# Windowed attention and a feed-forward block on one core: the score products of four heads issued as one group

## The chip, the core and the metric

The kernel runs on one core of one Trainium2 chip. The metric is the device time in microseconds (us) of one execution. The engines are TensorE (PE in the profile; its weight loads are PEld), VectorE (DVE), ScalarE (ACT), GpSimd (POOL) and SyncE (SP), which issues the DMAs. Each engine works through its own queue in the order in which the program issues to it.

## The reference

Attention in which a row sees 31 keys around it and, for each of the 24 blocks of 32 keys, one key (the maximum over the block) with the block's mean value; then layer norm and a two-layer feed-forward block on the result, in float32.

```python
def _attn_ref(q, k, v):                     # each (4, 8, 768, 64)
    B, H, S, D = q.shape
    block, window = (32, 16)
    nb = S // block
    scale = 1.0 / np.sqrt(D)
    k_sum = k.reshape(B, H, nb, block, D).max(axis=3)
    v_sum = v.reshape(B, H, nb, block, D).mean(axis=3)
    scores_l = scale * np.matmul(q, k.transpose(0, 1, 3, 2))
    mask_l = np.abs(pos[:, None] - pos[None, :]) < window
    scores_s = scale * np.einsum('bhsd,bhnd->bhsn', q, k_sum) + np.log(block)
    scores_l_m = np.where(mask_l, scores_l, -1000000000.0)
    a = softmax(np.concatenate([scores_l_m, scores_s], axis=-1))    # written out in full, with 1e-09 in the divisor
    return np.matmul(a, np.concatenate([v, v_sum], axis=2))

def _moe_ref(x, g_ln, w_ch1, w_ch2):        # x (4, 768, 512), w_ch1 (512, 2048), w_ch2 (2048, 512)
    xn = (x - mu) / np.sqrt(var + 1e-06) * g_ln
    return x + np.maximum(xn @ w_ch1, 0.0) @ w_ch2
```

Queries and keys are drawn eight times as large as the values. The result has the shape (4, 768, 512).

## The kernel before

The 4 x 768 rows are cut into 24 tiles of 128 rows, six for each batch. The eight heads of a tile are done in two half tiles of four heads, so there are 48 half tiles, numbered t; t = 0 to 11 are batch 0, t = 12 to 47 are batches 1 to 3. Two tiles (256 rows) make a group g of the feed-forward block, so there are 12 groups.

Batch 0 (`early_k`, `early_qk`, `early_transp`, `early_pv`) works in float32 while weights are loaded and converted. For t = 12 and up, `attend(t)` records these steps:

- `load_q(t)` brings the queries (buffer `qs`) and splits them into two float16 parts (`qhl`).
- `load_k(t, pr)`, once for each pair pr of heads, brings 184 key columns for each head into the single buffer `ksg`, has GpSimd put in the 24 block keys, has ScalarE make the high part `kh` and VectorE the low part `kl`. `kh` has one buffer for each pair, `kl` two in all.
- `qk(t, pr)` makes the scores of the two heads: two float16 products for each head, against `kh` and `kl`, into one PSUM tile `s` (two such tiles exist).
- `softmax(t, pr)`: VectorE adds the mask and finds the row minimum of the negated scores for each head, GpSimd scales the minimum (`mn`), ScalarE takes the exponential of each head.
- `load_v(t)`, `transp(t)` (the weights `p` in float16 parts, transposed by a DMA into `pT`) and `pv(t)` (twelve float16 products into PSUM `o`).

The feed-forward block is `g1(s)`, s = 8 g + j: 24 products of 256 columns into PSUM `h` (two runs of 12), then `g2(s)`: 12 products of 512 columns into the accumulators `a` of the group's two tiles (two runs of 6). Its operands are 32 bits wide (float32r).

The order in which all this is issued is not that of the code. `Plan.record` collects every instruction as an operation; instructions inside one `with pl.unit()` become one operation that is not broken up. `Plan.schedule` then lays the operations out on the engines with fixed costs, 24 times forwards and backwards, and `Plan.issue` keeps the layout whose modelled end is earliest and issues in that order. One draw of random numbers (`SEED`, `SPREAD = 2000.0`) shifts the first ranking by up to 2000 ns for each step. The model charges TensorE `SWITCH` = 93 ns where an operation differs from the one before it in `half`, which marks the score products of batch 0, whose contraction is 64 deep.

```python
if e == "tensor" and self.ops[i].half != half:
    half, t = self.ops[i].half, t + self.SWITCH
```

Every instruction is issued from one line of the helper, so the profile shows line 284 for all; the tile names tell them apart.

Of the kernel before, what the change touches and what calls it, by code (L numbers as in the profile page):

```python
# [16 lines left out]
F16 = mybir.dt.float16  # L17
# [7 lines left out]
P = 128  # L25
# [5 lines left out]
NC = 184  # L31
# [8 lines left out]
EH = 4  # L40
BS = 3
ROUNDS = 24
SEED, DRAWS = 2, 1
SPREAD = 2000.0
WARMQ = 4
WARMV = 4
# [17 lines left out]
class Plan:  # L64
# [58 lines left out]
    def record(self, engine, op, a, k):  # L123
        on_chip = lambda x: isinstance(x, bass.AP) and x.space != bass.MemoryType.DRAM
        outs = [x for x in (a[0], k.get("accum_out"), *a[7:8]) if on_chip(x)]
        ins = [x for x in (*a[1:7], *k.values()) if on_chip(x)]
        i, after = len(self.ops) - bool(self.joined), {}
        for aps, write in ((ins, False), (outs, True)):
            for x in aps:
                tile, *b = self.box(x)  # L130
                assert self.uses.get(tile, 1), tile
                if tile not in self.uses:
                    self.uses[tile] = []
                    if tile in self.prev:
                        for _, w, j in self.uses[self.prev[tile]]:
                            after[j] = after.get(j, False) or not w
                        self.uses[self.prev[tile]] = None
                elif tile in self.prev:
                    after.setdefault(self.uses[tile][0][-1], False)
                for c, w, j in self.uses[tile]:  # L140
                    if (write or w) and b[0] < c[1] and c[0] < b[1] and b[2] < c[3] and c[2] < b[3]:
                        after[j] = after.get(j, False) or not (write and w)
                self.uses[tile].append((b, write, i))
        busy, moving = self.cost(engine, op, a, k, ins, outs)
        columns = 0
        if engine == "tensor":
            columns = ({'matmul': 4, 'transpose': 2}[op] if ins[-1].dtype == F32 else 1) * math.prod(n for _, n in a[0].ap[1:]) * ins[0].ap[0][1] / P
        if self.joined:
            x = self.ops[i]
            x.calls.append((op, a, k))  # L150
            x.after.update(after)
            x.busy += busy
            x.columns += columns
        else:
            half = engine == "tensor" and ins[0].ap[0][1] == P // 2
            x = SimpleNamespace(engine=engine, calls=[(op, a, k)], after=after, busy=busy, moving=moving, columns=columns, stage=self.stage, port=self.port(engine, op, ins, outs), half=half)
            self.ops.append(x)
        x.after.pop(i, None)
        if self.joined is None:
            self.joined = True  # L160
# [44 lines left out]
    def schedule(self, rank, after, back):  # L205

        count = len(self.ops)
        before = [[] for _ in range(count)]
        left = [len(x) for x in after]
        for i, x in enumerate(after):  # L210
            for j, wait in x:
                before[j].append((i, wait))
        ready, start, end = [0.0] * count, [0.0] * count, [0.0] * count
        free = dict.fromkeys(self.ENGINES, 0.0)
        coming, waiting = ({e: [] for e in self.ENGINES} for _ in range(2))
        ring, warm, columns, tick = 0.0 if back else self.FIRST, False, 0.0, 0.0
        port, half = 0.0, False
        for i in range(count):
            if not left[i]:
                heapq.heappush(coming[self.ops[i].engine], (0.0 if back else 1000.0, i))  # L220
        for _ in range(count):
            t, e = min(
                (free[e] if waiting[e] else max(free[e], coming[e][0][0]), k)
                for k, e in enumerate(self.ENGINES)
                if waiting[e] or coming[e]
            )
            e = self.ENGINES[e]
            while coming[e] and coming[e][0][0] <= t:
                i = heapq.heappop(coming[e])[1]
                heapq.heappush(waiting[e], (rank[i], i))  # L230
            i = heapq.heappop(waiting[e])[1]
            busy, moving = self.ops[i].busy, self.ops[i].moving
            if self.ops[i].port:
                t = port = max(t, port)
                port += busy
            if e == "tensor" and self.ops[i].half != half:
                half, t = self.ops[i].half, t + self.SWITCH
            if e == "tensor" and not back:
                while t >= tick + self.TICK:
                    warm, columns, tick = columns >= 3200, 0.0, tick + self.TICK  # L240
                busy *= 1 if warm else 2
                at, per = t, self.ops[i].columns / busy
                while t + busy >= tick + self.TICK:
                    columns += (tick + self.TICK - at) * per
                    warm, columns, tick = columns >= 3200, 0.0, tick + self.TICK
                    at = tick
                columns += (t + busy - at) * per
            start[i], free[e], end[i] = t, t + busy, t + busy
            if e == "sync":
                ring = max(ring, t if back else t + busy + self.SETUP) + moving  # L250
                if back:
                    free[e] = max(free[e], ring)
                end[i] = ring + (self.SETUP + busy if back else 0)
            for j, wait in before[i]:
                ready[j] = max(ready[j], end[i] + wait)
                left[j] -= 1
                if not left[j]:
                    heapq.heappush(coming[self.ops[j].engine], (ready[j], j))
        return start, end
# [29 lines left out]
def body(ctx: ExitStack, tc, qt, qa, qe, kt, ks, va, vb, vs, g_ln, w1, w2, blocks, out):  # L289
# [8 lines left out]
    def psum(tag, name, shape):  # L298
        return pl.tile(pools[tag], shape, F32, tag, name, 2)
# [16 lines left out]
    nc = pl  # L316
# [187 lines left out]
    st = {}  # L504
# [43 lines left out]
            )  # L548

    @pl.step  # L550
    def qk(t, pr):
        qhl = st[t, "q"]
        kh, kl = st[t, "k", pr]
        ps = psum("s", f"s{t}_{pr}", [P, 2, NC])
        with pl.unit():
            for u in range(2):
                nc.tensor.matmul(ps[:, u, :], qhl[:, 2 * pr + u, :], kh[:, u, :], start=True, stop=False)
                nc.tensor.matmul(ps[:, u, :], qhl[:, 2 * pr + u, :], kl[:, u, :], start=False, stop=True)
        st[t, "s", pr] = ps

    @pl.step
    def softmax(t, pr):
# [54 lines left out]
    @pl.step  # L617
    def early_k(t):
        T, hh = divmod(t, 2)
        w = P * T  # L620
        for v in range(2):
            src, m, x = k0[2 * hh + v], bt["m", 0][:, 2 * hh + v], kx[t % 2][:, v]
            if v == 0:
                nc.scalar.copy(x[:, :NW], src[:, w : w + NW])
                nc.gpsimd.tensor_copy(x[:, P + BLK : P + BLK + NB], m)
            else:
                nc.scalar.copy(x[:, D:], src[:, w : w + P])
                nc.gpsimd.tensor_copy(x[:, : NW - P], src[:, w + P : w + NW])
                nc.gpsimd.tensor_copy(x[:, BLK : BLK + NB], m)
# [17 lines left out]
    @pl.step  # L647
    def early_transp(t, pr):
        p = st[t, "p"][:, 2 * pr : 2 * pr + 2].rearrange("p j c -> p (j c)")
        ps = psum("h" if t < EH else "s", f"pp{t}_{pr}", [P, 3, P])  # L650
        with pl.unit():
            for i in range(3):
                nc.tensor.transpose(ps[:, i, :], p[:, i * P : i * P + P], ident[:])
        e = work(f"v16_{pr}", f"pT{t}_{pr}", [P, 3, P])
        nc.scalar.copy(e[:], ps[:])
        st[t, "pt", pr] = e
# [205 lines left out]
    def attend(t):  # L862
        if t < NEARLY:
            early_k(t)
            early_qk(t)
            for pr in range(2):
                softmax(t, pr)
            for pr in range(2):
                early_transp(t, pr)
                early_pv(t, pr)  # L870
        else:
            load_q(t)
            for pr in range(2):
                load_k(t, pr)
                qk(t, pr)
                softmax(t, pr)
            load_v(t)
            transp(t)
            pv(t)
        if t % 2 and t < 8:  # L880
            norm(t // 2)

    def norm(T):
        ln(T)
        lnT(T)
# [26 lines left out]
    for t in range(NEARLY):  # L912
        if t % 2 == 0:
            fetch_tail(t // 2)
        attend(t)
# [13 lines left out]
    for t in range(8, 2 * TT + 1):  # L929
# [7 lines left out]
        b, i = divmod(t, 2 * NT)  # L937
# [66 lines left out]
```

## Time and profile before

| what | value |
|---|---|
| median of 3 runs | 683.55 us (682.82 to 685.04) |
| profiled execution | 682.88 us |
| its span, first to last instruction | 680.8 us |
| TensorE busy | 655.8 us (96%) |
| VectorE busy | 511.7 us (75%) |
| ScalarE busy | 369.8 us (54%) |
| GpSimd busy | 218.6 us (32%) |
| mean granted TensorE clock | 0.99 |

The profiled execution is 2.08 us longer than its span. A matmul's duration in the profile holds its way through the array, so neighbours overlap: what a product costs in a full queue is the distance from its start to the next one's start, and sums below are made of such distances. Times in a timeline are microseconds from the start of the span.

### The profile page before, as it was taken

The page shows a single profiled execution, that of the slowest core. Times are in us where ns is not written, and L with a number is a line of the kernel's source. Part 1 is how long each engine was busy: PE and PEld are TensorE (multiplying, and loading weights), DVE is VectorE, ACT ScalarE, POOL GpSimd, SP SyncE. Part 2 cuts the span into 40 slices and gives each one's busy share as a digit, 9 for nine tenths or more (in the row PEclk, how much of TensorE's full clock was granted, in tenths as well). Part 3 has the DMA queues.
Part 4 walks back from the last instruction along what each step waited for, and adds up shares of the span by engine and source line. Part 5 has one row for each costly group of instructions (what it writes and reads, how often), then busy time and mean ns, then how long its engine had stood idle before and what let it go on. Part 6 is the DMA issues. An engine that isn't in the chain of part 4 may idle for free.

```text
span 680.8 us, 13615 instructions
## 1 busy us (share of the span) xinstructions
PE 655.8 (96%) x4641; PEld 577.8 (85%) x4641; DVE 511.7 (75%) x1370; ACT 369.8 (54%) x970; POOL 218.6 (32%) x421
## 2 busy tenths in 40 slices
PE   9959999999999999989999999899999999999998
PEld 6748898888988987878988888798989888989997
DVE  3899989877566899879999888898998574742211
ACT  3936788475566766666666555666664434311110
POOL 4211200233333444634444354355343332310000
PEclk9959999999999999999999999999999999999999
DMA  9990564446564655655664544564543321210000
GB/s 304 362 350 28 147 214 121 146 138 183 141 164 121 176 139 128 170 151 150 172 141 126 141 102 101 126 146 103 144 108 81 84 79 35 55 24 1 32 1 31
DMA packets 109495, 87.89 MB, mean 129 GB/s; under 512 B 63218, under 2 KB 93938, under 8 KB 109427
## 3 DMA queue, kind: packets, MB, share of 16 engines
q1 hardware_dynamic: 109426, 87.04, 47.0%
q8 instruction: 36, 0.59, 0.4%
q14 instruction: 33, 0.26, 0.1%
HBM read 66.27 MB, written 6.29 MB: 107 GB/s over the span
## 4 chain that ended last, share of the span: by engine, by line
PE 43%; DVE 18%; DMA 13%; ACT 6%; issue 6%; POOL 2%; SPq 1%; ACTq 0%; POOLq 0%; DVEq 0%
PE h L284 20%; PE a L284 19%; DVE xn L284 4%; DMA ksg<-in_kt 4%; DMA bst<-in_vs 3%; DVE kl L284 2%; DMA bst<-in_qa 2%; ACT p L284 2%; DVE hl L284 2%; PE s L284 2%; PE o L284 1%; DVE p L284 1%; DVE v L284 1%; DVE vsum L284 1%; DVE x L284 1%
## 5 line engine op out<-in xcount | busy, mean ns | idle before, releaser
L284 PE MATMUL h<-xth,w 128*128 128x256 f32 x1536 | 301.3, 286 | 0.9 <-ACT xth L284 0.7
L284 PEld LDWEIGHTS h<-xth,w 128*128 128x128 f32 x1536 | 246.0, 190 | 4.1 <-ACT xth L284 1.1
L284 PE MATMUL a<-w,hh 128*128 128x512 f32 (+1 forms) x768 | 241.6, 396 | 0.0
L284 PE MATMUL h<-xtl,w 128*128 128x256 f32 x768 | 216.9, 282 | 0.8 <-POOL xtl L284 0.7
L284 PEld LDWEIGHTS a<-w,hh 128*128 128x128 f32 x768 | 135.4, 188 | 24.2 <-issue 0.9
L284 PE MATMUL a<-w,hl 128*128 128x512 f32 (+1 forms) x384 | 149.9, 390 | 0.2 <-DVE hl L284 0.2
L284 PEld LDWEIGHTS h<-xtl,w 128*128 128x128 f32 x768 | 145.8, 190 | 3.3 <-POOL xtl L284 1.0
L284 DVE SCALAR_TENSOR_TENSOR hl<-h,hh 128x512 fp32r<-128x512 f32 x96 | 65.7, 685 | 71.6 <-ACT hh L284 71.0
L284 ACT ACTIVATE hh<-h 128x512 fp32r<-128x512 f32 x96 | 56.5, 588 | 97.3 <-PE a L284 39.3
L284 ACT ACTIVATE p<-p,mn,sv 128x184 f32<-128x184 f32 x144 | 76.5, 532 | 57.7 <-POOL mn L284 57.5
L284 PEld LDWEIGHTS a<-w,hl 128*128 128x128 f32 x384 | 72.2, 188 | 16.9 <-DVE hl L284 0.6
L284 POOL TENSOR_TENSOR p<-p,p 128x512 f16<-128x512 f32 x72 | 71.6, 1002 | 39.6 <-ACT p L284 39.0
L284 DVE STREAM_TRANSPOSE xn<-xn 32x128 f32<-32x128 f32 x256 | 77.5, 303 | 4.5
L284 ACT ACTIVATE kh<-ksg,sv 128x368 f16<-128x368 f32 x72 | 43.2, 599 | 50.5 <-POOL ksg L284 39.3
L284 DVE SCALAR_TENSOR_TENSOR kl<-ksg,sv,kh 128x368 f16<-128x368 f32 x72 | 50.3, 699 | 20.8 <-ACT kh L284 20.0
L284 POOL TENSOR_SCALAR mn<-mn,sv 128x2 f32<-128x2 f32 x72 | 30.7, 427 | 78.5 <-DVE mn L284 69.1
L284 DVE CUSTOM_DVE_ANT_0 p<-s,mask 128x184 f32<-128x184 f32 x144 | 44.7, 340 | 9.9 <-PE s L284 9.2
L284 ACT ACTIVATE bst<-bst 128x384 f32<-128x384 f32 (+2 forms) x55 | 32.5, 590 | 26.8 <-DMA bst<-in_qa 11.6
L284 POOL COPY ksg<-ksum 128x48 f32<-128x48 f32 x72 | 18.8, 261 | 84.1 <-DMA ksg<-in_kt 66.1
L284 DVE SCALAR_TENSOR_TENSOR v<-vst,sv,v 128x256 f16<-128x256 f32 x72 | 42.5, 612 | 1.7 <-ACT v L284 1.2
L284 DVE SCALAR_TENSOR_TENSOR wf<-raw,wf 128x512 uint32<-128x512 uint32 x64 | 41.8, 680 | 0.0
L284 POOL TENSOR_TENSOR x<-x,rc 128x256 f32<-128x256 f32 x36 | 25.2, 699 | 47.6 <-DVE x L284 44.0
(106 smaller groups left out, 818.3 us busy)
## 6 DMA issues: line engine op xcount, KB each, us to landing
raw<-in_w SPq DMA_DIRECT2D x32, 512.0 KB
ksg<-in_kt SPq DMA_DIRECT2D x72, 184.0 KB
qs<-in_qt SPq DMA_DIRECT2D x72, 128.0 KB
out_x<-x SPq DMA_DIRECT2D x23, 256.0 KB
vst<-in_va SPq DMA_DIRECT2D x36, 128.0 KB
bst<-in_ks SPq DMA_DIRECT2D x20, 192.0 KB
bst<-in_qa SPq DMA_DIRECT2D x15, 256.0 KB
bst<-in_vs SPq DMA_DIRECT2D x20, 192.0 KB
```

The costliest lines, as they stand in the source:

```text
L284: getattr(getattr(nc, self.ops[i].engine), op)(*a, **k)
```

## The change

In `attend(t)`, for batches 1 to 3, the two `qk(t, pr)` become one `qk(t)` behind both `load_k`: its eight products are one unit, so nothing can stand between the first pair's and the second pair's, and both PSUM tiles `s` are taken together. The products themselves are the same. The planner's `half` gets three values: 1 for the score products of batch 0, 2 for other float16 products (`qk` and `pv`), 0 for the rest. 93 ns are now also charged where TensorE goes from float16 products to others, but not for the way in. The random seed goes from 2 to 8. Since the order of all engines comes out of the planner, all of them get a new order.

```diff
--- before.py
+++ after.py
@@ -40,7 +40,7 @@
 EH = 4
 BS = 3
 ROUNDS = 24
-SEED, DRAWS = 2, 1
+SEED, DRAWS = 8, 1
 SPREAD = 2000.0
 WARMQ = 4
 WARMV = 4
@@ -152,7 +152,7 @@
             x.busy += busy
             x.columns += columns
         else:
-            half = engine == "tensor" and ins[0].ap[0][1] == P // 2
+            half = engine == "tensor" and (1 if ins[0].ap[0][1] == P // 2 else 2 * (ins[-1].dtype == F16))
             x = SimpleNamespace(engine=engine, calls=[(op, a, k)], after=after, busy=busy, moving=moving, columns=columns, stage=self.stage, port=self.port(engine, op, ins, outs), half=half)
             self.ops.append(x)
         x.after.pop(i, None)
@@ -214,7 +214,7 @@
         free = dict.fromkeys(self.ENGINES, 0.0)
         coming, waiting = ({e: [] for e in self.ENGINES} for _ in range(2))
         ring, warm, columns, tick = 0.0 if back else self.FIRST, False, 0.0, 0.0
-        port, half = 0.0, False
+        port, half = 0.0, 0
         for i in range(count):
             if not left[i]:
                 heapq.heappush(coming[self.ops[i].engine], (0.0 if back else 1000.0, i))
@@ -234,7 +234,8 @@
                 t = port = max(t, port)
                 port += busy
             if e == "tensor" and self.ops[i].half != half:
-                half, t = self.ops[i].half, t + self.SWITCH
+                t += self.SWITCH if self.ops[i].half + half != 2 or not self.ops[i].half else 0
+                half = self.ops[i].half
             if e == "tensor" and not back:
                 while t >= tick + self.TICK:
                     warm, columns, tick = columns >= 3200, 0.0, tick + self.TICK
@@ -548,15 +549,16 @@
             )
 
     @pl.step
-    def qk(t, pr):
-        qhl = st[t, "q"]
-        kh, kl = st[t, "k", pr]
-        ps = psum("s", f"s{t}_{pr}", [P, 2, NC])
+    def qk(t):
+        ps = [psum("s", f"s{t}_{pr}", [P, 2, NC]) for pr in range(2)]
         with pl.unit():
-            for u in range(2):
-                nc.tensor.matmul(ps[:, u, :], qhl[:, 2 * pr + u, :], kh[:, u, :], start=True, stop=False)
-                nc.tensor.matmul(ps[:, u, :], qhl[:, 2 * pr + u, :], kl[:, u, :], start=False, stop=True)
-        st[t, "s", pr] = ps
+            for pr in range(2):
+                for u in range(2):
+                    for n, k in enumerate(st[t, "k", pr]):
+                        q = st[t, "q"][:, 2 * pr + u, :]
+                        nc.tensor.matmul(ps[pr][:, u, :], q, k[:, u, :], start=(n == 0), stop=(n == 1))
+        for pr in range(2):
+            st[t, "s", pr] = ps[pr]
 
     @pl.step
     def softmax(t, pr):
@@ -872,7 +874,8 @@
             load_q(t)
             for pr in range(2):
                 load_k(t, pr)
-                qk(t, pr)
+            qk(t)
+            for pr in range(2):
                 softmax(t, pr)
             load_v(t)
             transp(t)
```

Three places show it. First, TensorE in half tile 26 (a name such as s26_0 is a PSUM tile of half tile 26 and pair 0; a4_1 is the accumulator of group 4, tile 1; h40 is block 40 of the first layer). Before, the second pair's scores stand by themselves:

```order
L284 MATMUL a4_1_660<-w2_11_326,hl37_675 128x512
L284 LDWEIGHTS qhl26_858
L284 MATMUL s26_1_868<-kh26_1_866,qhl26_858 128x184
L284 LDWEIGHTS qhl26_858
L284 MATMUL s26_1_868<-kl26_1_867,qhl26_858 128x184
L284 LDWEIGHTS qhl26_858
L284 MATMUL s26_1_868<-kh26_1_866,qhl26_858 128x184
L284 LDWEIGHTS qhl26_858
L284 MATMUL s26_1_868<-kl26_1_867,qhl26_858 128x184
L284 MATMUL a4_0_659<-w2_12_332,hh38_677 128x512 x2
```

Now they follow the first pair's directly:

```order
L285 LDWEIGHTS qhl26_858
L285 MATMUL s26_0_865<-kh26_0_860,qhl26_858 128x184
L285 LDWEIGHTS qhl26_858
L285 MATMUL s26_0_865<-kl26_0_861,qhl26_858 128x184
L285 LDWEIGHTS qhl26_858
L285 MATMUL s26_1_866<-kh26_1_863,qhl26_858 128x184
L285 LDWEIGHTS qhl26_858
L285 MATMUL s26_1_866<-kl26_1_864,qhl26_858 128x184
```

The first pair's four products stood further up before, with 24 products of h and 12 of a between the pairs. Over the whole program TensorE's row goes from float16 products to others 103 times before and 68 times now.

Second, TensorE ahead of the attention output (o) of half tile 32. Before:

```order
L284 MATMUL h52_909<-xtl_6_855,w1_8_305 128x256
L284 MATMUL h52_909<-xth_6_854,w1_8_305 128x256 x2
L284 MATMUL h52_909<-xtl_6_855,w1_8_305 128x256
L284 MATMUL h52_909<-xth_6_854,w1_8_305 128x256
L284 LDWEIGHTS pT_32_1038
L284 MATMUL o32_1039<-v16_0_351,pT_32_1038 128x128
```

Now:

```order
L285 MATMUL a6_1_899<-w2_7_302,hh51_907 128x512 x2
L285 MATMUL a6_1_899<-w2_7_302,hl51_908 128x512
L285 MATMUL a6_0_898<-w2_8_308,hh52_910 128x512 x2
L285 MATMUL a6_0_898<-w2_8_308,hl52_911 128x512
L285 MATMUL a6_0_898<-w2_9_314,hh52_910 128x512 x2
L285 MATMUL a6_0_898<-w2_9_314,hl52_911 128x512
L285 LDWEIGHTS pT_32_1038
L285 MATMUL o32_1039<-v16_0_351,pT_32_1038 128x128
```

Before, o32 stood behind the first half of h52 of the feed-forward block; now it stands behind h52's second layer for one tile. So more feed-forward products stand ahead of the same attention step. Counted from the program's start, the products of h and a ahead of a step are:

| ahead of | h before | h now | a before | a now |
|---|---|---|---|---|
| o28 | 1104 | 1128 | 528 | 540 |
| o32 | 1260 | 1308 | 600 | 630 |
| o35 | 1380 | 1440 | 666 | 684 |
| o44 | 1872 | 1824 | 900 | 888 |
| s32, second pair | 1224 | 1272 | 576 | 600 |

On VectorE, ahead of the low part kl of the second pair of half tile 32, stand ten more 32-row transposes (xn) and two more hl than before, and two fewer row minima (p).

Third, SyncE at the start of the program (in_ks are the keys of batch 0, four loads; in_va its values; in_qe its queries). Before:

```order
L284 DMA spare2_10_94<-in_va 128x2x256
L284 DMA spare1_13_89<-in_ks 128x768
L284 DMA spare2_12_88<-in_ks 128x768
L284 DMA spare2_11_95<-in_va 128x2x256
L284 DMA blk_84<-in_blocks 128x144
L284 DMA spare2_10_94<-in_va 128x2x256
L284 DMA spare1_12_87<-in_ks 128x768
L284 DMA spare2_11_95<-in_va 128x2x256
L284 DMA spare1_10_91<-in_qe 128x512
L284 DMA spare2_13_90<-in_ks 128x768
```

Now:

```order
L285 DMA spare2_10_94<-in_va 128x2x256 x2
L285 DMA blk_84<-in_blocks 128x144
L285 DMA spare1_12_87<-in_ks 128x768
L285 DMA spare2_12_88<-in_ks 128x768
L285 DMA spare1_13_89<-in_ks 128x768
L285 DMA spare1_10_91<-in_qe 128x512
L285 DMA spare2_13_90<-in_ks 128x768
L285 DMA spare2_11_95<-in_va 128x2x256 x2
```

Four loads of values stood ahead of the last key load, now two. On TensorE two of the calls v0 (the block means of the values, two products each) ahead of the first score products of batch 0 have moved behind them. On VectorE three more instructions stand ahead of the first hl.

## The prediction, written before the changed kernel was run

> **What bounds the kernel now.** I read the page's engine shares and slices first.
>
> ```profile
> span 680.8 us, 13615 instructions
> PE 655.8 (96%) x4641; PEld 577.8 (85%) x4641; DVE 511.7 (75%) x1370; ACT 369.8 (54%) x970; POOL 218.6 (32%) x421
> PE   9959999999999999989999999899999999999998
> DVE  3899989877566899879999888898998574742211
> PEclk9959999999999999999999999999999999999999
> ```
>
> TensorE bounds the program: its digit is 8 or 9 in all 40 slices but the third, and its clock's is 9 in all but that one. So the change can win in two ways only, fewer TensorE nanoseconds or fewer TensorE waits. The windows view says where it waits (time, then busy time of PE, PEld, DVE, ACT, POOL, clock, DMA):
>
> ```profile
> 15.00:45.00 30.00, 21.59 (x150) 16.13 (x150) 27.41 (x90) 22.53 (x78) 7.06 (x19) 0.83 1.06 367
> 45.00:140.00 95.00, 92.67 (x639) 82.48 (x639) 89.28 (x225) 65.18 (x197) 14.67 (x36) 0.98 0.46 141
> 140.00:250.00 110.00, 109.69 (x798) 97.28 (x798) 78.06 (x202) 70.98 (x183) 38.52 (x74) 1.00 0.60 155
> 250.00:430.00 180.00, 171.21 (x1249) 149.21 (x1249) 160.87 (x457) 113.93 (x288) 81.53 (x142) 1.00 0.55 137
> 430.00:500.00 70.00, 70.00 (x522) 62.31 (x521) 64.61 (x172) 41.94 (x100) 34.04 (x54) 1.00 0.52 129
> ```
>
> From 140 to 250 and from 430 on TensorE has no idle time worth a term. From 250 to 430, the middle of the attention of batches 1 to 3, it idles 180.00 - 171.21 = 8.79 us. The waits of TensorE in that window (us in all, times, longest) name the cause:
>
> ```profile
> PE o L284 <- DMA pT<-p: 4.5, 5, 2.2
> PE s L284 <- DVE kl L284: 2.5, 4, 1.7
> PE h L284 <- POOL xtl L284: 0.7, 1, 0.7
> PE vps L284 <- DVE vm L284: 0.5, 1, 0.5
> PE s L284 <- ACT kh L284: 0.3, 1, 0.3
> PE a L284 <- DVE hl L284: 0.2, 1, 0.2
> ```
>
> Sum 8.7 us, of which 7.3 us are attention steps (o, s) that came to the head of TensorE's queue before their data. The feed-forward products queued behind them had nothing to wait for: the queue is in order, so an attention step placed too early stops work that was ready.
>
> **The change, part by part: switches.** A stretch of TensorE's timeline with no wait in it:
>
> ```profile
> 399.15 0.40 PE L284 MATMUL a<-w,hl 128*128 128x512 f32 x1
> 399.39 0.26 PE L284 MATMUL s<-kh,qhl 128*128 128x184 f16 x1
> 399.48 0.24 PE L284 MATMUL s<-kl,qhl 128*128 128x184 f16 x1
> 399.56 0.24 PE L284 MATMUL s<-kh,qhl 128*128 128x184 f16 x1
> 399.64 0.24 PE L284 MATMUL s<-kl,qhl 128*128 128x184 f16 x1
> 399.67 0.37 PE L284 MATMUL h<-xth,w 128*128 128x256 f32 x1
> 399.87 0.28 PE L284 MATMUL h<-xtl,w 128*128 128x256 f32 x1
> ```
>
> and two runs of the chain of waits that give the plain distances:
>
> ```profile
> 80.06 1.41 PE a L284 x6
> 85.88 1.41 PE h L284 x12
> ```
>
> A product of a takes 1.41 / 6 = 0.235 us, of h 1.41 / 12 = 0.1175, of s 0.08 (399.48 to 399.56). Going in: 399.15 to 399.39 is 0.24, 0.005 over a; the first s takes 0.09, 0.01 over. Going out: from the last s (399.64) to the second h (399.87) are 0.23, where 0.08 + 0.1175 = 0.198 would do, 0.033 over. A visit to float16 products costs 0.048 us beside the products. The order has 103 such visits before and 68 now: 35 x 0.048 = **1.7 us less**. The products are the same in number and form, so nothing else of TensorE's own work changes. The bounds are narrow, 1.3 to 2.0 us with 0.01 us of rounding on each visit.
>
> **The middle stage.** The new order puts more feed-forward work ahead of the attention steps there: ahead of o32 48 products of h and 30 of a more, 48 x 0.1175 + 30 x 0.235 = 12.7 us; some 20 visits fewer by then take off 1.0 us, which leaves 11.7. Ahead of o28 it is 24 and 12 (5.6 us), ahead of o35 60 and 18 (11.3 us). VectorE, which feeds these steps, has its part pushed back less. Ahead of the second kl of half tile 32 stand ten more transposes, two more hl and two fewer row minima; by the groups of the page
>
> ```profile
> L284 DVE STREAM_TRANSPOSE xn<-xn 32x128 f32<-32x128 f32 x256 | 77.5, 303 | 4.5
> L284 DVE SCALAR_TENSOR_TENSOR hl<-h,hh 128x512 fp32r<-128x512 f32 x96 | 65.7, 685 | 71.6 <-ACT hh L284 71.0
> L284 DVE CUSTOM_DVE_ANT_0 p<-s,mask 128x184 f32<-128x184 f32 x144 | 44.7, 340 | 9.9 <-PE s L284 9.2
> L284 ACT ACTIVATE p<-p,mn,sv 128x184 f32<-128x184 f32 x144 | 76.5, 532 | 57.7 <-POOL mn L284 57.5
> ```
>
> 10 x 0.303 + 2 x 0.685 - 2 x 0.340 = 3.7 us. For the scores of that half tile's second pair, with 48 h and 24 a more ahead, the slack grows by 11.3 - 1.0 - 3.7 = 6.6 us. That is about as much as TensorE lost by waiting over the whole stage, so most of these waits could go: at most 8.8 us.
>
> Against it stand two things. Grouping delays the first pair: its row minima and exponentials, which now overlap the wait for the second pair's keys, come bunched behind the eighth product. Per half tile that is two minima and two exponentials more between the second kl and pT, 2 x 0.340 + 2 x 0.532 = 1.7 us. And VectorE itself: it is busy 160.87 of the 180 us. Where TensorE is never idle (430 to 500) VectorE runs at 64.61 / 70.00 = 92.3%; if that is what it can do beside a full TensorE, the stage needs 160.87 / 0.923 = 174.3 us, and 5.7 of the 8.8 us can be had. The lower end is no gain. I take half of 8.8, **4.4 us less**: nearer to VectorE's bound than to nothing, because the slack is counted, and less than it, for the 1.7 us.
>
> **The start.** TensorE's and VectorE's rows there:
>
> ```profile
> 8.59 3.60 PE L284 MATMUL v<-spare,blk 128*120 128x512 f32 x8
> 12.03 0.27 PE L284 MATMUL s<-ident 128*128 128x128 f32 x1
> 11.65 0.95 DVE L284 TENSOR_REDUCE kmax<-spare 128x24 f32<-128x768 f32 x1 [1.42 <-DMA spare<-in_ks]
> 42.13 1.12 PE L284 MATMUL tx<-ident,xn 128*128 128x128 f32 x4 [5.79 <-DVE xn L284]
> 43.92 0.58 PE L284 MATMUL h<-xth,w 128*128 128x256 f32 x1 [0.68 <-ACT xth L284]
> 44.65 0.58 PE L284 MATMUL h<-xtl,w 128*128 128x256 f32 x1
> ```
>
> Four of the eight products of v, (12.03 - 8.59) / 2 = 1.7 us, move behind the first scores, and two value loads behind the last keys. So VectorE, busy 27.41 of 30 us from 15 to 45 and awaited by TensorE at 42.13, can begin up to 1.7 us sooner. Against it, VectorE has three more instructions ahead of the first hl, by the rows above up to 3 x 0.95 = 2.9 us. Net -1.7 to +1.2; I take **0.5 us less**.
>
> Every other engine's order is new too, but GpSimd (32%) and ScalarE (54%) have room, and from 500 us on the rest is TensorE's own work. I cost that at nothing; the cover is that idle time, and without it a wait of the size of the present ones, 0.5 to 2 us each, comes in.
>
> **Sum.** 682.88 (the profiled execution: span 680.8 and 2.08 around it) - 1.7 - 4.4 - 0.5 = 676.3. The median of the runs shown is 683.55, 0.67 above that execution, so I forecast **677 us**.
>
> **Rivals.** (1) Only the switches are won. The attention chain is as late as before in relation to TensorE's row, because the bunched 1.7 us eat the new slack; waits in the middle stay at 8.8 us, perhaps in other places. 683.55 - 1.7 = 681.9. For it: the plan's slack before was also laid out to suffice and did not. Against: 6.6 us of slack at half tile 32 against 1.7 us of delay.
>
> (2) Slower: the group waits for the later kl with all eight products, and o for a pT that is 1.7 us later. It decides where the planner's room between the scores and o is tight: in the five half tiles where o waits now. If ten of the some 15 half tiles from 250 to 430 wait the 1.7 us in full and nothing is recovered, that is +17, less the 8.8 that may go and the 1.7 of switches: 683.55 + 6.5 = 690. It needs waits of o on pT of some 17 us in all. For it: o <- pT is already the largest wait. Against: ahead of o32 stand 11.7 us more work.
>
> (3) A long wait that also halves the clock. After the 5.79 us wait at 42.13 two h products start 44.65 - 43.92 = 0.73 apart and the clock slice reads 5; the waits of at most 2.2 us in the middle leave it at 9. A wait of 6 us at a group there would cost its 6 and as much again if the following 6 us ran at half speed: 683.55 - 1.7 + 6 + 3 = 691. The Trainium skill ("TensorE: Matmul & The Clock Gate", "Why this matters for your kernels") warns of idle gaps over about 3 us between bursts, after which the clock is halved; the trace agrees at 5.79 us and shows no wait between 2.2 and 5.8 in which to test that limit. By that rule alone a wait of 3.5 us would be enough.
>
> That the change does not do what it says is excluded: the order shows the pairs together.
>
> **Chances.** Forecast (the middle stage's waits partly or mostly go, 670 to 681): 0.65. Rival 1: 0.19. Rival 2: 0.13. Rival 3: 0.03. A measurement of this kernel tells 0.3%, 2 us, from no change, so faster is below 681.5 and slower above 685.6. Rival 1 lies at 681.9, on the edge: 0.04 of its 0.19 I give to faster, 0.13 to same, 0.02 to slower, as the start may cost 1.2. With 0.01 of rival 2 as same: faster 0.69, same 0.14, slower 0.17. The range: the low end is the forecast with all waits gone and the start's best, 683.55 - 2.0 - 8.8 - 1.7 = 671.0; the upper end takes in rival 1 with the start's worst and new waits of 2 us, 683.55 - 1.3 + 1.2 + 2 = 685.5. The forecast's own range is 671 to 681.
>
> **What would show it.** Right: about 4 us of idle TensorE in the stretch that answers to 250 to 430, fewer waits o <- pT and s <- kl, and half as many visits with the same 0.048 us each; VectorE at 92% or more there. Wrong: o <- pT above 4.5 us (rival 2), TensorE's idle time the same with other names (rival 1), a 5 in the clock row after the third slice (rival 3), or a first h well after 43.92. If a visit's cost does not stand in the four-head group as it does here, the switch term is wrong.

## Result and the profile after

The changed kernel takes **692.76 us** (median of 4 executions, 692.34 to 696.59); the kernel before took 683.85 us beside it (median of 4, 682.82 to 685.04). The ratio is **1.0142, 95% interval [1.0102, 1.0182]**: slower, by 1.4%. The forecast was 677 us, faster; the time lies above the range as well.

The profiled execution of the change took 696.59 us (span 694.5), which is 3.8 above its median and 13.7 above the profiled execution before. The page's shares and slices, to be laid beside those of the kernel before:

```profile
span 694.5 us, 13580 instructions
PE 658.4 (95%) x4641; PEld 582.5 (84%) x4641; DVE 517.6 (75%) x1370; ACT 367.9 (53%) x970; POOL 217.7 (31%) x421
PE   8869899999999989989989999999999999999998
DVE  4899889885557799978898889779998893832111
PEclk9969999999999999999999999999999999999999
```

The number of products is the same (x4641) and their busy time nearly so (658.4 for 655.8). What TensorE does not do has grown: 694.5 - 658.4 = 36.1 us of idle time, where it was 680.8 - 655.8 = 25.0. So 11.1 of the 13.7 us are waits; the other 2.6 are busy time, to which the clock belongs (see the switches below). The windows view (time, busy time of PE, PEld, DVE, ACT, POOL, clock, DMA) says where:

```profile
15.00:45.00 30.00, 21.21 (x145) 15.51 (x144) 27.46 (x91) 21.64 (x73) 4.26 (x17) 0.86 1.06 373
45.00:140.00 95.00, 91.37 (x620) 81.56 (x620) 86.55 (x212) 63.98 (x193) 15.90 (x34) 0.95 0.46 138
140.00:250.00 110.00, 107.75 (x754) 95.24 (x753) 73.68 (x189) 68.63 (x178) 36.09 (x69) 1.00 0.59 150
250.00:430.00 180.00, 169.01 (x1227) 149.55 (x1226) 159.06 (x428) 106.50 (x269) 76.50 (x131) 0.99 0.51 126
430.00:500.00 70.00, 66.55 (x492) 59.32 (x491) 58.97 (x166) 38.06 (x94) 30.12 (x52) 1.00 0.48 117
```

| stretch (us) | idle before | idle after |
|---|---|---|
| 15 to 45 | 8.41 | 8.79 |
| 45 to 140 | 2.33 | 3.63 |
| 140 to 250 | 0.31 | 2.25 |
| 250 to 430 | 8.79 | 10.99 |
| 430 to 500 | 0.00 | 3.45 |

No stretch gained. The middle, where 4.4 us should have come back, lost 2.2 more, and the stretches on both sides of it, which had next to no waits from 140 to 250 and from 430 to 500, have them now. In the slower kernel the same stretch of time holds somewhat earlier work; between the starts of o20 and o35, which is the same attention work in both, TensorE idles 8.7 us before and 11.8 after. Who is waited for, from 45 us to the end (waits view of TensorE: us in all, times, longest):

```profile
PE o L285 <- DMA pT<-p: 7.2, 7, 2.3
PE s L285 <- DVE kl L285: 5.0, 7, 1.0
PE s L285 <- DVE xtl L285: 1.8, 2, 1.5
PE s L285 <- ACT kh L285: 1.5, 1, 1.5
PE vps L285 <- DVE vm L285: 1.4, 1, 1.4
PE a L285 <- DVE hl L285: 1.2, 1, 1.2
```

For the most part they are the same two attention steps as before, o (for the transposed weights) and s (for the keys): 16.3 us with all waits of o and s, where the kernel before has 8.6 from 45 us on. The planner's order calls them up before their data are there, only more often.

### The profile page after: what moved, and what is told of

It is laid out like the page before. It is cut to its first block, busy times and chain, and to the rows that moved or that the text cites. A ratio compares the mean times of both kernels' runs of the same rounds, so it can differ in the third digit from the quotient of the medians.

```text
span 694.5 us, 13580 instructions
## 1 busy us (share of the span) xinstructions
PE 658.4 (95%) x4641; PEld 582.5 (84%) x4641; DVE 517.6 (75%) x1370; ACT 367.9 (53%) x970; POOL 217.7 (31%) x421
## 4 chain that ended last, share of the span: by engine, by line
PE 36%; DVE 7%; DMA 4%; ACT 2%; issue 2%; SPq 1%; POOL 1%; POOLq 0%; ACTq 0%; DVEq 0%
PE a L285 17%; PE h L285 16%; DMA ksg<-in_kt 3%; DVE xn L285 1%; DVE kl L285 1%; PE s L285 1%; PE o L285 1%; SPq L285 1%; DVE v L285 1%; PE last L285 1%; ACT p L285 1%; ACT kh L285 1%; DVE hl L285 1%; DVE qhl L285 1%; DMA bst<-in_vs 1%
## 5 line engine op out<-in xcount | busy, mean ns | idle before, releaser
L285 ACT ACTIVATE qhl<-qs,sv 128x512 f16<-128x512 f32 x36 | 25.9, 720 | 48.3 <-PE s L285 33.9
L285 POOL COPY ksg<-ksum 128x48 f32<-128x48 f32 x72 | 22.0, 306 | 85.7 <-DMA ksg<-in_kt 63.5
L285 DVE CUSTOM_DVE_ANT_0 p<-s,mask 128x184 f32<-128x184 f32 x144 | 42.2, 342 | 7.8 <-PE s L285 7.6
L285 POOL TENSOR_SCALAR mn<-mn,sv 128x2 f32<-128x2 f32 x72 | 25.0, 348 | 72.6 <-DVE mn L285 68.8
L285 DVE SCALAR_TENSOR_TENSOR v<-vst,sv,v 128x256 f16<-128x256 f32 x72 | 44.9, 641 | 0.9 <-ACT v L285 0.5
```

What stands on the lines that cost most here:

```text
L285: getattr(getattr(nc, self.ops[i].engine), op)(*a, **k)
```

## Experiments

The short theory names in the quoted expectations: G is that the group itself slows the attention, S that the order of loads on SyncE does, C or L that the planner's new charge does, GC that the charge does so only together with the group, O or D that every new order is a draw. A "visit" is one stay of TensorE at float16 products. Ratios are to the kernel before, run beside each.

### The parts of the change apart

**Seed 8 alone, pairs split, old charge.**

```diff
-SEED, DRAWS = 2, 1
+SEED, DRAWS = 8, 1
```

> The kernel before with the seed of the change (8 for 2) and nothing else: pairs issued apart, old charge for switches. Theory G (the group itself slows the attention chain: eight products wait for the later kl, the first pair's softmax comes bunched): within 2 us of the kernel before, 682 to 686 us. Theory O (the newly drawn order is what costs, whatever stands in the group): clearly off the kernel before, 688 to 697 us if the seed alone does it; 97 visits to float16 products in place of 103 by its order, so 0.3 us less for these in either case.

Measured: 689.58 us, ratio 1.0081 [1.0055, 1.0106]. A new seed on the old kernel costs nearly 6 us by itself.

**The group with the old charge, seed 2, and then seed 8.** The edit is the change without its three lines on `half`, and for the first one without the new seed.

> The four heads as one group, but with the old seed and the old charge for switches. Theory G: as slow as the change, 690 to 695 us, with the load-to-load time of ksg about 0.5 us longer than before in the middle stage. Theory O: its order is a draw of its own, so it may land anywhere between 680 and 692; a time under 684 would be enough to drop theory G. 72 visits to float16 products: 1.5 us less than before for these in either case.

> Group with the old charge and seed 8: the fourth corner of seed by group under the old charge. If seed 8 is bad of itself: 689 to 694 us, the cost of the split kernel with seed 8 again. If every order is a draw of its own and the seed's number means nothing: anywhere from 683 to 693 us.

Measured: 685.17 us (1.0013 [0.9984, 1.0041]; 72 visits) and 683.89 us (1.0008 [0.9985, 1.0032]; 72 visits). All 36 pairs stand together in both, and both are level with the kernel before. So with these two seeds grouping, re-planned, costs nothing that can be told; and seed 8 is not bad in itself, as with the group it is no worse than seed 2. A third seed with the group, further down, took 691.18.

**The whole change with seed 2** (71 visits).

```diff
-SEED, DRAWS = 8, 1
+SEED, DRAWS = 2, 1
```

> The changed kernel with the old seed 2: group and new charge for switches, 71 visits to float16 products. The seed alone cost 5.8 us with split pairs (689.6 against 683.8) and the group alone nothing (685.2). Theory O (the drawn order costs, not the group): 680 to 687 us. If the new charge is what costs: as slow as the change, 690 or more.

Measured: 697.54 us, 1.0190 [1.0160, 1.0219]. With either seed, group and new charge together are 9 to 12 us above the group with the old charge, at the same number of visits (68 and 71 against 72).

### Holding an order still

Two kernels keep an order and move only the scores, in the first one with the softmax behind them, after the plan is made.

**The old order, pairs joined**: in the kernel before, the first pair's products and softmax are moved to just ahead of the second pair's, where no dependency forbids it. 17 pairs end up joined, and the visits go from 103 to 87.

```diff
+        for ours, theirs in zip(first, second):
+            for e in self.ENGINES:
...
+                new[at:at] = mine
```

> The order of the kernel before, kept on all engines, but in the 16 half tiles where it can be done without turning round a dependency the first pair's scores and softmax are moved to just ahead of the second pair's. 17 pairs then stand together and 87 visits remain of 103. Theory G: 16 of 36 half tiles grouped, so about 16/36 of the 10.6 us that the change lost beyond its switches, +4.7, less 0.8 us of switches: 687 to 689 us. Theory O: only the switches, 16 x 0.048 = 0.8 us less, 682 to 684 us.

Measured: 687.99 us, 1.0070 [1.0042, 1.0099]. In an order that was laid out for two separate pairs the joining costs some 4 us, although it saves 16 visits.

**The new order, pairs opened**: in the change, the first pair's four products go one run of feed-forward products earlier (103 visits again).

```diff
+            for j in early.get(i, ()):
+                for op, a, k in self.ops[j].calls[:4]:
+                    getattr(nc.tensor, op)(*a, **k)
```

> The order of the changed kernel, kept on all engines, but in 35 or 36 half tiles the first pair's four products are issued one feed-forward run (some 1.4 us) earlier on TensorE, so the pairs stand apart again: 103 visits in place of 68. Theory G: the first pair no longer waits for the second pair's kl, so a good part of the loss comes back, 686 to 692 us. Theory O: the loss stays and the visits come on top, 35 x 0.048 = 1.7 us, 693 to 696 us.

Measured: 693.33 us, 1.0138 [1.0092, 1.0185], the change's own time. Taking the pairs apart again doesn't bring back the time: the loss sits in the order around them.

### A rival on SyncE

In the changed order SyncE holds many loads of values (`vst`) ahead of the key loads (`ksg`). Its own waits from 250 to 430 had grown, before and after:

```profile
SPq L284 <- ACT v L284: 8.3, 7, 1.9
```

```profile
SPq L285 <- ACT v L285: 21.0, 12, 4.1
```

Two kernels put a value load that stands up to three places ahead of a key load behind it, 73 loads in the new order and 80 in the old.

```diff
+            for j in reversed(queue):
+                if not load(j).startswith("vst"):
+                    continue
...
+                new.insert(new.index(i) + 1, j)
```

> The order of the changed kernel; on SyncE alone, value loads (vst) that stand among the three issues ahead of a key load (ksg) are put behind it: 73 value loads move. Theory S (the key loads wait in SyncE's queue behind value loads that wait for ScalarE's conversions, 21.0 us of such waits from 250 to 430 against 8.3 before, and this lengthens the ring of key loads to 13.0 us a half tile): the ring falls to about 12.2 us and the time by 4 to 8 us, 685 to 689 us. If these waits only stand where the queue would wait anyway: within 1.5 us of the change, 691 to 694 us.

> The same edit on the order of the kernel before (80 value loads move). Theory S: TensorE waits less in the middle stage, 678 to 682 us. Otherwise within 1.5 us of the kernel before, or slower, if values then come late.

Measured: 694.62 us (1.0156 [1.0132, 1.0179]) and 682.61 us (0.9993 [0.9972, 1.0015]). Nothing came back, although in the first of them SyncE's wait for v from 250 to 430 fell from 21.0 to 4.2 us (its waits for kl and for the keys' own loads grew). And the group with the old charge and seed 8 has 19.1 us of the same wait and is level with the kernel before. So these longer waits on SyncE are not what costs the time.

### The charge, or a draw

What was left is the planner's new charge: 93 ns for every return from float16 products, where the trace shows 0.033 us for it. It went alone into the kernel before (pairs split), with both seeds, and a third seed was tried with the group.

```diff
-            half = engine == "tensor" and ins[0].ap[0][1] == P // 2
+            half = engine == "tensor" and (1 if ins[0].ap[0][1] == P // 2 else 2 * (ins[-1].dtype == F16))
...
-                half, t = self.ops[i].half, t + self.SWITCH
+                t += self.SWITCH if self.ops[i].half + half != 2 or not self.ops[i].half else 0
+                half = self.ops[i].half
```

> The kernel before with the planner's new charge alone (93 ns where TensorE leaves float16 products; pairs split, seed 2; 96 visits). Theory C (the charge makes the slow orders: both orders with group and charge are 9 to 12 us over those with group and the old charge): 690 to 697. Theory D (every order is a draw, of no part of the change): anything between 682 and 697, so below 687 speaks for D. Theory GC (the charge costs only together with the group, where it pulls the eight products to another float16 product): 682 to 686.

> The same with seed 8 (pairs split, new charge; 94 visits). Seed 8 with split pairs and the old charge took 689.6. Theory C: 9 to 12 over that, 697 to 702, or at the least above 692. Theory D: 682 to 697, with no relation to 689.6. Theory GC: about 689.6, within 3.

> Group with the old charge, a third seed (5; 70 visits). Theories C and GC: like the other two with the old charge (685.2 and 683.9), 682 to 687. Theory D: 682 to 697.

> Group with the new charge, the third seed (5; 70 visits). Theories C and GC: 9 to 12 over the same seed with the old charge, 691 to 699. Theory D: 682 to 697; at or below the same seed with the old charge makes D the likelier.

Measured, with the ones above (us):

| | old charge | 93 ns | difference |
|---|---|---|---|
| split, seed 2 | 682.92 (the kernel before, beside it) | 686.59 (1.0060 [1.0037, 1.0082]) | +3.7 |
| split, seed 8 | 689.58 | 695.29 (1.0177 [1.0146, 1.0208]) | +5.7 |
| group, seed 2 | 685.17 | 697.54 | +12.4 |
| group, seed 8 | 683.89 | 692.76 (the change) | +8.9 |
| group, seed 5 | 691.18 (1.0110 [1.0071, 1.0149]) | 688.60 (1.0090 [1.0062, 1.0118]) | -2.6 |

Four of five say that the charge costs, also without the group, which is against GC; but 686.59 lies under the 690 of theory C, under the 687 that was to speak for D, and only 0.6 above the range of GC. The fifth pair says the opposite, which by what was expected makes D the likelier, and 683.9, 685.2 and 691.2 for one and the same rule show how far a draw alone moves the time. Five pairs could not settle it, so the charge was given in doses, everything else as in the change.

```diff
-                t += self.SWITCH if self.ops[i].half + half != 2 or not self.ops[i].half else 0
+                t += 0 if self.ops[i].half == 2 and not half else CHARGE if half == 2 and not self.ops[i].half else self.SWITCH
```

> The change with a charge of -93 ns instead of 93 for leaving float16 products (72 visits): the plan thinks TensorE quicker and puts more feed-forward products ahead of each attention step. Theory L (the charge takes the cover away: 69 visits x 93 ns are 6.4 us fewer feed-forward products ahead of the last attention steps than TensorE has time for): fewer waits than with no charge (683.9), so 676 to 684. Theory D (a draw): 682 to 698, in no order.

> The same with seed 2 (71 visits), where no charge took 685.2. Theory L: 677 to 685. Theory D: 682 to 698.

> The change with a charge of 300 ns (69 visits; 69 x (300 - 93) = 14.3 us more of TensorE's time set aside in the plan). Theory L: well above the change's 692.8, 697 to 707. Theory D: 682 to 698.

> The same with seed 2 (69 visits), where 93 ns took 697.5. Theory L: 700 to 712. Theory D: 682 to 698.

> The change with a charge of -200 ns (71 visits). At -93 TensorE still waits 2.7 us for o and s. Theory L going on: 678 to 681. If the attention steps now come so late that the first feed-forward products of the next group wait for their rows (the waits of h): 683 to 688. Theory D: 682 to 698.

Measured. "Waits" are TensorE's waits of o and s from 45 us on (the last scores of batch 0 among them), added up from the waits view; "ahead of o40" are the TensorE products that stand ahead of the o step of half tile 40, counted by kind and taken at the plain distances of the prediction (0.1175 us for an h, 0.235 for an a, 0.08 for an s); the other kinds make 62 us of it in every kernel, so the differences are h, a and s.

| charge (ns) | seed 8: time | ratio | waits | ahead of o40 | seed 2: time | ratio | waits | ahead of o40 |
|---|---|---|---|---|---|---|---|---|
| -200 | 680.52 | 0.9957 [0.9937, 0.9978] | 3.8 | 471.8 | | | | |
| -93 | 681.63 | 0.9982 [0.9954, 1.0010] | 3.0 | 470.4 | 682.01 | 0.9984 [0.9964, 1.0005] | 3.9 | 471.8 |
| 0 | 683.89 | 1.0008 | 7.6 | 469.0 | 685.17 | 1.0013 | 5.6 | 469.0 |
| 93 | 692.76 | 1.0142 | 16.3 | 461.9 | 697.54 | 1.0190 | 12.6 | 466.1 |
| 300 | 696.99 | 1.0225 [1.0175, 1.0274] | 15.1 | 447.8 | 698.86 | 1.0241 [1.0203, 1.0279] | 10.1 | 449.9 |

With both seeds the time rises with the charge at every step, and the number of visits stays at 68 to 72. Only the step from 0 to 93 ns is beyond what can be told apart by itself; the intervals of every other pair of neighbours overlap. Of the waits with seed 8, the one of o shows it best. The two largest of TensorE's waits for the attention from 45 us on, at -93, 0 and 300 ns (seed 8; at 93 ns the wait of o is 7.2 us), each kernel by itself:

```profile
PE o L285 <- DMA pT<-p: 1.1, 3, 0.5
PE s L285 <- DVE kl L285: 1.0, 2, 0.7
```

```profile
PE o L284 <- DMA pT<-p: 4.4, 3, 2.4
PE s L284 <- DVE kl L284: 1.5, 3, 0.6
```

```profile
PE o L285 <- DMA pT<-p: 12.9, 11, 3.2
PE s L285 <- DVE kl L285: 1.3, 1, 1.3
```

The reading that fits this, in one sentence: what the plan charges for a switch and TensorE doesn't spend is feed-forward work missing ahead of the next attention step, so TensorE arrives early and, since its queue is in order, stands there. At 300 ns 21 us of products are gone from ahead of o40 against no charge.

The five pairs of the table before can be read the same way. Taken over the o steps of all 36 half tiles, 93 ns change the h and a work that stands ahead of a step, on the mean, by -2.2 us (split, seed 2), -0.7 (split, seed 8), -1.2 (group, seed 2), -2.5 (group, seed 8) and +0.2 (group, seed 5). So the one pair in which the charge did not cost is the one in which it took no work away. The waits of o and s rise in all five pairs, in that one too (9.2 to 13.1 us); there TensorE's other waits from 45 us on fell by more, from 9.4 to 3.2.

Three limits. The sign goes with the time, the size doesn't: -1.2 us of work goes with +12.4 us, -2.5 with +8.9. At 300 ns the time came out just under what theory L expected (697 to 707, and 700 to 712), and the waits of o and s are no larger than at 93 ns, with seed 2 smaller (12.6 to 10.1); with seed 8 the rest went to other waits (23.7 us for all of TensorE's from 45 us on, against 21.3 in the change). And the work ahead of o40 orders kernels only within one rule: the kernel before has just 450.6 us there, less than the change, and waits 8.6 us for o and s.

### What the group itself is worth

**Pairs split, charge -93 ns, seed 2** (98 visits, against 71 with the group).

> Pairs split as in the kernel before, charge -93 ns, seed 2 (98 visits, 27 more than the group with the same charge and seed, which took 682.0). If the group is worth its switches, 27 x 0.048 = 1.3 us more: 683.3. If the group's bunching costs as much as its switches save: 682. If the group is what hurts: 678 to 681.

Measured: **680.18 us, 0.9951 [0.9931, 0.9971]**. The split kernel with a negative charge beats the kernel before, and the group with the same charge and seed (682.01) is not clear of it. So the 27 visits that the group saves buy nothing that shows in the time. 680.18 lies where it was expected if the group is what hurts, but the two are one draw each and 1.8 us apart, so that isn't shown either. This kernel and the group at -200 ns (680.52) are the quickest of all that ran, about 3 us under the kernel before, and level with each other. In both, TensorE's idle time from 250 to 430 shrank from the 8.79 us before to 180.00 - 173.63 = 6.4 and 180.00 - 173.30 = 6.7 (the group with the old charge and seed 8, level with the kernel before, has 180.00 - 174.43 = 5.6 there, so this stretch alone doesn't make the time):

```profile
250.00:430.00 180.00, 173.63 (x1277) 152.60 (x1276) 162.72 (x463) 115.80 (x294) 81.54 (x142) 1.00 0.55 138
```

```profile
250.00:430.00 180.00, 173.30 (x1269) 153.93 (x1268) 154.68 (x443) 108.08 (x272) 79.79 (x137) 1.00 0.54 132
```

## Why the prediction was wrong

**The switches: the mechanism held, the time was lost elsewhere.** A visit in the changed kernel with no wait in it, from the timeline (of its eight products the first two and the last):

```profile
422.81 0.28 PE L285 MATMUL h<-xth,w 128*128 128x256 f32 x1
422.93 0.25 PE L285 MATMUL s<-kh,qhl 128*128 128x184 f16 x1
423.02 0.24 PE L285 MATMUL s<-kl,qhl 128*128 128x184 f16 x1
423.49 0.24 PE L285 MATMUL s<-kl,qhl 128*128 128x184 f16 x1
423.52 0.71 PE L285 MATMUL a<-w,hh 128*128 128x512 f32 x2
424.07 0.40 PE L285 MATMUL a<-w,hl 128*128 128x512 f32 x1
```

In, 0.12 for an h of 0.1175; the first s takes 0.09; out, 423.49 to 424.07 is 0.58 where 0.08 + 2 x 0.235 = 0.55 would do. Within the rounding that is the 0.048 us of the prediction, and there are 35 visits fewer, which is worth 1.7 us. TensorE's busy time rose all the same, by 2.6 us, because it worked longer at a halved clock. The stretches in which the granted clock is 0.50 while there is work, before (one) and after (three), in the windows view:

```profile
35.01:48.66 13.65, 6.61 (x27) 5.52 (x28) 13.65 (x27) 4.54 (x9) 3.10 (x2) 0.50 1.05 371
```

```profile
36.71:50.36 13.65, 7.65 (x33) 6.96 (x34) 13.65 (x27) 4.86 (x9) 0.79 (x2) 0.50 1.03 349
84.50:87.91 3.41, 3.41 (x16) 2.97 (x17) 3.40 (x13) 2.52 (x11) 0.49 (x3) 0.50 0.47 144
360.98:364.39 3.41, 3.41 (x12) 2.89 (x11) 3.35 (x12) 2.12 (x5) 1.87 (x4) 0.50 0.70 141
```

TensorE was busy in them for 6.6 us before and 14.5 after. Half of the 7.9 us more is 3.9 us of time, an estimate that takes the work at 0.50 for twice as long; without it TensorE's work fell by 3.9 - 2.6 = 1.3 us, near the 1.7. So the switches were won and paid over several times: 11.1 us of waits and 3.9 of halved clock.

**The middle stage: this is the step that failed, the slack that was counted ahead of the attention steps.** The term was -4.4 us and came out at +2.2 from 250 to 430, +1.9 from 140 to 250 and +3.5 from 430 to 500. It said that 11.7 us more of TensorE's work ahead of o32 are slack, because VectorE's part of half tile 32 is pushed back by 3.7 us only. The keys' low parts (VectorE) and the second pair's first product (TensorE) of half tile 32, before:

```profile
386.97 0.60 DVE L284 SCALAR_TENSOR_TENSOR kl<-ksg,sv,kh 128x368 f16<-128x368 f32 x1 [0.79 <-ACT kh L284]
388.50 0.24 PE L284 MATMUL s<-kh,qhl 128*128 128x184 f16 x1
```

and after:

```profile
410.26 1.26 DVE L285 SCALAR_TENSOR_TENSOR kl<-ksg,sv,kh 128x368 f16<-128x368 f32 x1 [0.29 <-ACT kh L285]
411.08 0.24 PE L285 MATMUL s<-kh,qhl 128*128 128x184 f16 x1
411.57 0.24 PE L285 MATMUL s<-kl,qhl 128*128 128x184 f16 x1 [0.25 <-DVE kl L285]
```

The second kl ends at 387.57 before and at 411.52 after, 24 us later, not 3.7. TensorE came to these scores 22.6 us later and still had to wait. Of o32's own delay (401.2 to 426.4 us, 25.2) the products ahead make 12.7, as counted. The other 12.5 are time that TensorE lost on the way: it idled 28.3 us ahead of o32 where it had idled 18.7, which is 9.6 more, 6.1 of them already ahead of o20; the halved clock took 3.9 more; and the visits that are gone give back 1.0. The prediction compared one place of VectorE's queue with one place of TensorE's and took everything upstream as fixed. VectorE had 3.7 us more to do ahead of that kl and came to it 24 us later, so it too was held up by others on the way. Extra feed-forward work ahead of an attention step therefore didn't tell how much room the step had; that it tells how late the plan expected the step's data is a reading that no run tests by itself. The kernel with charge -93 (seed 8) shows what room looks like at the same half tile:

```profile
399.47 0.85 DVE L285 SCALAR_TENSOR_TENSOR kl<-ksg,sv,kh 128x368 f16<-128x368 f32 x1 [0.25 <-ACT kh L285]
405.14 0.26 PE L285 MATMUL s<-kh,qhl 128*128 128x184 f16 x1
```

There the keys are ready 4.8 us before the group begins.

**The order as a whole, costed at nothing: failed too.** The prediction read the change as eight products moved together, and weighed the new charge and the new seed only through the order they made, place by place; all that it didn't follow it costed at nothing, for the room on GpSimd and ScalarE. The charge runs show a cost of the plan's rule with two seeds: 683.89 to 692.76 with seed 8, 685.17 to 697.54 with seed 2. They show just as well that a draw is worth 6 to 7 us (683.9, 685.2 and 691.2 for the group with the old charge; 689.6 for the split pairs with seed 8, where the kernel before has 683.8 with seed 2). A range that allowed new waits of 2 us in all was too narrow for an order that is new on five engines.

**VectorE's bound** (92.3% beside a full TensorE) decided nothing: in the middle VectorE did 159.06 us after, against 160.87, while TensorE idled more.

**The start** came as said for its milestone and not for its sum. TensorE's first h began at 43.12 instead of 43.92, after a shorter wait:

```profile
41.33 1.11 PE L285 MATMUL tx<-ident,xn 128*128 128x128 f32 x4 [4.98 <-DVE xn L285]
43.12 0.58 PE L285 MATMUL h<-xth,w 128*128 128x256 f32 x1 [0.68 <-ACT xth L285]
```

But less had been done by then: TensorE's idle time from 15 to 45 is 0.4 us higher, and the clock stayed at 0.50 until 50.36 instead of 48.66 us, so it is no gain.

**The rivals.** (1), only the switches are won, didn't come: they were won, and more was lost. (2), slower by a later pT, named the right wait and the right side, but that its 690 lies near is luck. It needed some 17 us of these waits, and o <- pT rose from 4.5 to 7.2; and its sum takes off 8.8 us that may go where it says that nothing is recovered, without which it gives 683.55 + 17 - 1.7 = 698.9. Nor does the bunching of the group make the wait, since the group with the old charge waits 4.4 and 5.0 us for pT and is level with the kernel before. Where the old order was held still, bunching did cost (687.99); a re-plan absorbed it. (3), a halved clock after a long wait: the clock was halved two times more than before, after much shorter waits than the 6 us it priced, which is worth the 3.9 us above. It is not what sets the slow orders apart, as the group with the old charge and seed 2 has 18.1 us of work at the halved clock and took 687.40 in that execution. Nor is it shown to be why the profiled execution is 3.8 us above the median: another one had a lower mean clock (0.983 against 0.985) and took 693.10. The row that spoke for this rival was read wrongly, too. In the kernel before the clock stands at 0.50 from 35.01 us, and the wait of 5.79 us that was to have halved it begins only at 42.13 - 5.79 = 36.34, so that trace shows no halving by a wait of this length.

**What stays open.** How much of this one order's 8.9 us is the charge and how much its luck: seed 5 came out the other way, and a single draw can't be split. Why a charge below nothing does no worse than none, and at -200 ns a little better: the doses fit a plan that is too hopeful about the engines that feed the attention, which a negative charge makes up for, but that was not measured apart. A charge of the measured 0.03 to 0.05 us wasn't run, and the doses were run with two seeds only.

## What to carry to other kernels

When a planner makes the order, an edit to its costs is an edit to every engine: run the same edit with several seeds, and the parts of the change apart, before giving the time to any one instruction that moved. In an in-order queue, work that stands ahead of a step is slack only against the time at which the step's data really come, so read that time from the data's own engine in both orders. And a cost that a plan charges and the chip doesn't spend isn't the safe side: with two seeds of three it cost 9 and 12 us here, and the reading that fits is that it takes away the work that would have covered the next wait.

## What the runs showed of the hardware

TensorE's clock was halved after short waits, and not only in the changed kernel. In the kernel before it stands at 0.50 from 35.01 us, after waits of 0.94 us (to 34.13) and before the one of 0.44 us (to 35.44) and the one of 5.79 us; the long wait falls into a stretch that was already at half. The second of the two places that the changed kernel adds, in slices of a microsecond (windows view; the clock is the number after POOL's), and the products ahead of it:

```profile
357.67 0.24 PE L285 MATMUL s<-kl,qhl 128*128 128x184 f16 x1
359.39 0.24 PE L285 MATMUL s<-kh,qhl 128*128 128x184 f16 x1 [1.48 <-ACT kh L285]
360.50 0.24 PE L285 MATMUL s<-kl,qhl 128*128 128x184 f16 x1 [0.87 <-DVE kl L285]
```

```profile
360.00:361.00 1.00, 0.50 (x4) 0.46 (x4) 1.00 (x2) 0.06 (x1) 1.00 (x1) 0.99 1.08 268
361.00:362.00 1.00, 1.00 (x4) 0.80 (x3) 1.00 (x2) 0.66 (x1) 0.59 (x1) 0.50 1.30 244
362.00:363.00 1.00, 1.00 (x4) 0.81 (x3) 0.97 (x9) 0.05 (x1) 0.27 (x1) 0.50 0.93 199
363.00:364.00 1.00, 1.00 (x6) 0.90 (x6) 0.97 (x2) 1.00 (x4) 0.96 (x2) 0.50 0.14 33
364.00:365.00 1.00, 1.00 (x8) 1.00 (x8) 1.00 (x2) 1.00 (x5) 0.03 (x1) 0.81 0.02 8
365.00:366.00 1.00, 1.00 (x18) 0.96 (x17) 0.74 (x3) 1.00 (x5) 0.00 (x0) 1.00 0.74 172
```

Two waits of 1.48 and 0.87 us with one short product between them, 2.6 us with next to no work, and then 3.4 us at 0.50 (360.98 to 364.39), which costs about 1.7, the same estimate as above. The other place, half from 84.50, follows a single wait of 1.50 us that ends at 84.33. A wait of 2.3 us for pT in the same execution (the longest of the seven above, to 300.75) left the clock alone, so the length of one wait doesn't decide it; what does, the runs don't show. The Trainium skill ("TensorE: Matmul & The Clock Gate", "Why this matters for your kernels") warns of gaps over about 3 us; here the clock was halved after less.
